# A spectral layer with gated feed-forward on one core: new order of the filter stage, late half evacuations, a moved table load

## The chip, the cores and the metric

The kernel runs on 1 core of one Trainium2 chip. The metric is the device time of one execution in microseconds. The engines are named as in the profile: PE is TensorE, PEld its weight loads, DVE is VectorE, ACT is ScalarE, POOL is GpSimd, SP is SyncE. SP and POOL also issue the DMAs here; SPq and POOLq are their queues.

## The reference, cut to what matters

The input is one sequence of 2048 rows with 576 columns in bf16. First comes a layer norm, a two-dimensional real FFT over rows and columns, a product with a complex filter, and the inverse FFT; the result is added to the input. Then comes a layer norm and a gated feed-forward network with 4608 hidden columns, added again.

```python
def _A_ref(x, w_r, w_i):
    X = jnp.fft.rfft2(x.astype(jnp.float32), axes=(-2, -1))
    W = w_r + 1j * w_i
    X = X * W
    return jnp.fft.irfft2(X, s=(S, D), axes=(-2, -1)).astype(jnp.bfloat16)

def _B_ref(x, w_gate, w_up, w_down):
    return (_gelu(x @ w_gate) * (x @ w_up)) @ w_down

h = x + _A_ref(_layernorm(x), A_w_r, A_w_i)
h2 = h + _B_ref(_layernorm(h), B_w_gate, B_w_up, B_w_down)
```

## The kernel before, in words

**Infrastructure.** A small class `Prog` records every operation with the keys that it reads and writes, and turns them into semaphore waits. Each engine runs its operations in the order in which they are recorded. So the order of the work is the order of the lists below, and an operation that waits holds up everything behind it on its engine. A DMA is recorded on the queue that issues it, SP or POOL, and holds its place there in the same way.

**Stages.** The 2048 rows are 16 tiles of 128 (index c or n). Stage one (list SEQ1) normalises the rows and transforms them along the row axis into U, grouped in 16 groups of frequencies (index i or g). The filter stage (list SEQF) works group by group. The second block (list SEQ) transforms back, adds to the input, normalises, turns tiles 0 to 3 and starts the feed-forward. Tiles 8 to 15 are transformed back later, between the gate/up matmuls (`def_i`, `def_n`). The feed-forward fills the rest.

**The filter stage.** SEQF is written out by hand. A capital letter is the first part of a step, the small letter the second part and its evacuation from PSUM.

- D and d: the transform along the columns, 4 matmuls and then 6; evacuated to CUS by the engine in DENG[i] (line 650 for the matmuls).
- B: 4 matmuls that combine the rows' parts; evacuated to YS by BENG[i] (line 670).
- T: the filter product on DVE, a large multiply into TP (columns 0 to 255) and a small one into TR (the remaining 32 columns) (line 683).
- V and v: the first inverse step on TP, 8 matmuls each; evacuated to V by the engines in VENG[i], one engine for both banks or one for each (line 691).
- R and r: the same for the remainder columns, one step for four groups, from TR (line 708). R0, R1 and R2 are evacuated to RB by RENG and copied to VR by eight DMAs each, shared between SP and POOL. R3 is evacuated by eight small copies straight into VR.

The evacuations are all recorded by one helper, line 616, and the DMAs by line 242. PSUM has 8 banks, used as 4 pairs. A step takes the pair that has been out of use longest (`FB`, `used`, `busy`).

**The second block.** I and i are the second inverse step of a tile, with the V weights and, at the end of i, with the VR weights (line 839). E is the evacuation to GS (lines 845, 846 and 616). N and o are the inverse transform along the rows with the table IT (line 856), a is the addition to XO on DVE (line 862). s, q and c are the variance, the root and its reciprocal; n is the normalisation to HN (line 890; P in its name puts it on POOL); u and U turn HN on PE (line 908), e is that evacuation to HT. G0 and G1 are the first gate/up matmuls (line 948). The bank pairs are chosen in the same way (`SLOT`, `last`, `held`). The loads of the first gate/up weights are issued on SP at the tokens named in LOADS.

**Where the table comes in.** IT and the identity IDT are loaded on SP early, behind the filter weights WS, the tables VT and DT, and ahead of the small loads `w_zero` of WS.

Of the kernel before, what the change touches and what calls it, by code (L numbers as in the profile page):

```python
# [12 lines left out]
NZ, NY = 5, 3  # L13
ABASE = 1
FF = 4608
NT = 16
# [13 lines left out]
DENG, BENG = ['act', 'dve', 'act', 'act', 'act', 'act', 'act', 'act', 'dve', 'act', 'act', 'act', 'act', 'act', 'act', 'act'], ['act', 'dve', 'act', 'act', 'act', 'act', 'act', 'dve', 'act', 'act', 'act', 'act', 'act', 'act', 'act', 'act']  # L30
LOADS = {".I0": "a0 a1 a2 a3 a4 a5", ".N0": "b0", ".i3": "b1", ".o1": "b2", ".N3": "b3", ".o3": "b4 b5", ".i7": "d"}
RENG = ['dve', 'act', 'act', 'act', 'act']
QR = ((0, 1), (1, 2), (2, 3), (3, 4), (4, 8), (8, 16))
DEF0, DSTEP = 3, 4
SEQ = """I0 I1 I2 i0 E0S i1 E1S i2 E2A N0 I3 o0 i3 N1 I4 o1 a0 E3S N2 o2 a1 s0A q0 i4 a2 s1A I7 c0 N3 E4S q1 s2D i7 I6 o3 E7A i6 c1 N4 o4 a3 q2 E6A c2 N7 I5 o7 a4 n0P N6 s3A a7 i5 n1P n2P q3 c3 o6 u1 U1 u2 E5A u0 U2 a6 n3P e1A e2D U0 N5 u3 e0A o5 a5 U3 G0 e3D G1""".split()

# [10 lines left out]
def build_tables():  # L47
# [106 lines left out]
    assert np.allclose(VN[0, 0], VN[0, 1])  # L154
    T["VTAB"] = np.stack([v if k else v.reshape(128, 4, 16, 4).transpose(0, 1, 3, 2).reshape(128, 256) for v, k in ((VN[0, 0], 1), (VN[0, 0], 0), (VN[1, 0], 1), (VN[1, 1], 1), (VN[1, 0], 0), (VN[1, 1], 0))], 1).reshape(128, -1)

# [175 lines left out]
def _build(nc, A_x, A_w_r, A_w_i, B_w_gate, B_w_up, B_w_down, out):  # L332
# [78 lines left out]
    TR = sb.alloc("TR", [128, 2, 2, 2, 128], BF16)  # L411
    RB = sb.alloc("RB", [128, 3, 2, 2, 4, NT], BF16)

# [18 lines left out]
    P.op(POOL, lambda g: g.memset(EXQ[:, :], -0.5), w=["EXQ"])  # L432
    P.op(POOL, lambda g: g.memset(VR[:, :, :, :, :], 0.0), w=[("V", g, 2 + t) for g in range(NG) for t in range(2)])
    xv = A_x[0].rearrange("(p c) d -> p c d", c=NT)
# [105 lines left out]
    def a_bank(i, k):  # L540
        return (5 * i + AORD.index(k) + ABASE) % 8

# [57 lines left out]

    FB, used, busy = {}, {0: -8, 2: -7, 4: -6, 6: -5}, set()
    for t, w in enumerate(SEQF):
# [83 lines left out]
    def st_V(i, second, engs):  # L686
        g, z, b0 = GORD[i], i % NZ, FB["V", i]

        def mm(h, o, ct, first, last, after):
            c, t_ = ct  # L690
            return P.op(PE, lambda t: t.matmul(bank(b0 + o, 0, 128, 128 * c, 128 * c + 128), TP[64 * h:64 * h + 64, z, o, t_, c:256:2], VT[64 * h:64 * h + 64, 0 if g else 2 + o, t_, :],  # L691
                                               start=first, stop=last), r=[("T", z), "VT" if g else "VT2"], w=[("PS", b0 + o)], after=after)

        halves(("V", i), second, [[(c, t_) for c in range(2) for t_ in range(2)]] * 2, mm)
        if not second:
            return
        v5 = V[:, :, :, :, g, :, :].rearrange("p c t n j e -> p j (c t n) e")
        n = 2 // len(engs)
        for a, e in enumerate(engs):
            ev(e, v5[:, n * a:n * a + n], banks(b0 + a, n, 256).rearrange("p a (c e) -> p a c e", e=4), [("PS", b0 + a + k) for k in range(n)], [("V", g, a + k) for k in range(n)])  # L700

    def st_R(q, second):
# [12 lines left out]
        if q < 3:  # L715
            ev(RENG[q], RB[:, q, :, :, :, :].rearrange("p t o e n -> p o t (e n)"), banks(b0, 2, 128).rearrange("p o (t x) -> p o t x", t=2), keys, [("RB", q)])
            for j, i in enumerate(js):
                for t_ in range(2):
                    k = t_ if q == 2 else (2 * j + t_) % 3 > 0
                    P.dma((SP, POOL)[k], VR[64 * t_ + 32 * (j % 2):64 * t_ + 32 * (j % 2) + 32, GORD[i], :, :, :], RB[32 * j:32 * j + 32, q, t_, :, :, :], f"r{q}{k:d}", r=[("RB", q)], w=[("V", GORD[i], 2 + t_)])  # L720
            return
        for i in js:
            j, g = i % 4, GORD[i]
            for t_ in range(2):
                dst = VR[64 * t_ + 32 * (j % 2):64 * t_ + 32 * (j % 2) + 32, g, :, :, :].rearrange("p o e n -> p o (e n)")
                src = PS[32 * j:32 * j + 32, b0 * 512:(b0 + 2) * 512].rearrange("p (a c) -> p a c", a=2)[:, :, 128 * (i == LAST) + 64 * t_:128 * (i == LAST) + 64 * t_ + 64]
                ev((ACT, DVE, DVE, ACT)[j], dst, src, keys, [("V", g, 2 + t_)])

# [33 lines left out]
    def hold(eng=SP):  # L762
        P.op(eng, None, after=[P.ops[PE][-1]])

    def tab2_load():
# [13 lines left out]
    def loads(w):  # L779
        for v in LOADS.get(w, "").split():  # L780
            if v == "d":
                tab2_load()
            else:
                wg0_part(int(v[1]), *((0, 256, ["WGA"]) if v[0] == "a" else (256, 1152, [("WG", 0, i) for i in range(4)])))
# [24 lines left out]
    vk = [vmain, vmain, vtail]  # L809
    vkeys = vmain + vtail  # L810


    SLOT, last, held, ing = {}, [sorted(used.values()).index(used[2 * b]) - 4 for b in range(4)], set(), False
    for t, w in enumerate(SEQ):
# [6 lines left out]
        elif k in "ioUEae":  # L821
# [11 lines left out]
    def i_mm(c, second):  # L833
        b, e = SLOT["I", c], ends.setdefault(("I", c), [None, None])
        for j in range(2 + second):
            for r in range(2):
                o, r0 = r ^ (not second), 64 * r
                lhs = V[r0:r0 + 64, j, o, c, :, :, :] if j < 2 else VR[r0:r0 + 64, :, :, :, c].rearrange("p g o e -> p (g o e)")
                e[o] = P.op(PE, lambda t, r0=r0, o=o, j=j, lhs=lhs: t.matmul(bank(b + o, 0, 128, 0, KW), lhs, DT[r0:r0 + 64, 2 * o + j if j < 2 else 4, 0:KW], start=(not second and j == 0), stop=(second and j == 2)),  # L839
# [120 lines left out]
    def gu_first(i):  # L960
        for a in range(4):
# [29 lines left out]
    def def_i(c, second):  # L991
        e = ends.setdefault(("X", c), [None, None])
        for j in range(3):
            for r in range(2):
                o, r0 = r ^ (not second), 64 * r
                t_ = j if j < 2 else r
                lhs, rhs = (V[r0:r0 + 64, o, t_, c, :, :, :], DP[r0:r0 + 64, 2 * o + t_, :]) if j < 2 else (VR[r0:r0 + 64, :, :, :, c].rearrange("p g o e -> p (g o e)"), DP[r0:r0 + 64, 4 + o, :])
                e[o] = P.op(PE, lambda t, o=o, t_=t_, lhs=lhs, rhs=rhs, j=j: t.matmul(bank(6 + o, 0, 128, HK * t_, HK * t_ + HK), lhs, rhs, start=(not second and j == 0), stop=(second and j == 2)),  # L998
                            r=vk[o if j < 2 else 2] + ["DP"], w=[("PS", 6 + o)], after=[e[o]] if second and j == 0 else [])
        if not second:  # L1000
# [133 lines left out]
```

## Time and profile before

| what | us |
|---|---|
| median of 3 runs | 485.5 (485.09 to 485.71) |
| profiled execution, its own time | 484.82 |
| span of the profile | 483.0 |
| PE busy | 476.7 |
| DVE busy | 183.2 |
| ACT busy | 145.4 |
| POOL busy | 51.2 |

The profile is of one execution. Its span is from the first to the last instruction; the execution's own time is a little longer. A line of the chain of waits has the start, the length and what held the end up in that time. A line of a timeline has start, length, engine, source line, operation, output and inputs, shape, count, and in brackets the idle time before it with what ended it. In a group, busy time and the mean of one instruction in ns stand behind the bar, then the idle time before.

### The profile page before, as it was taken

Reading aid. Unit: us, or ns where it says so; the run is one execution under the profiler, and the core shown is the slowest. Engines: PE = TensorE matmul, PEld = TensorE weight load, DVE = VectorE, ACT = ScalarE, POOL = GpSimd, SP = SyncE. Lnnn points to the kernel's source line nnn. Section 1 sums busy time; section 2 is a strip of 40 time slices with the busy share of each in tenths; the row PEclk is TensorE's granted clock in tenths of the full one; section 3 lists DMA queues with packets and bytes.
Section 4 is the critical chain, followed back from the end, with each engine's and each line's share of the span. In section 5 each row is a group of like instructions: output and inputs, shape, how many; then the busy total and the mean of one; then the engine's idle time right before and its main releaser. Section 6 shows DMA issues by size and latency. Waiting matters only on the chain.

```text
span 483.0 us, 12887 instructions
## 1 busy us (share of the span) xinstructions
PE 476.7 (99%) x5873; PEld 289.0 (60%) x5874; DVE 183.2 (38%) x366; ACT 145.4 (30%) x291; POOL 51.2 (11%) x86
## 2 busy tenths in 40 slices
PE   7999999999999999999999999999999999999998
PEld 3877755555588644444688544444788444445884
DVE  7998655565500143333200244333101233333011
ACT  6998753434300022332100122233000232223000
POOL 7753317010120000000000000000000000000000
PEclk9999999999999999999999999999999999999999
DMA  8883878951520001000000011000000000000000
GB/s 292 226 219 70 278 248 289 375 104 27 195 88 17 26 18 23 18 1 0 3 14 15 26 24 23 12 0 2 3 14 27 14 1 0 1 1 1 3 26 26
DMA packets 28454, 33.19 MB, mean 69 GB/s; under 512 B 12656, under 2 KB 21488, under 8 KB 28400
## 3 DMA queue, kind: packets, MB, share of 16 engines
q1 hardware_dynamic: 24768, 19.88, 14.6%
q0 software_dynamic: 3632, 12.49, 7.9%
q8 instruction: 46, 0.75, 0.7%
q14 instruction: 8, 0.07, 0.0%
HBM read 26.21 MB, written 2.36 MB: 59 GB/s over the span
## 4 chain that ended last, share of the span: by engine, by line
PE 96%; DVE 1%; DMA 1%; POOL 1%; issue 0%; SPq 0%; POOLq 0%; DVEq 0%
PE PS L948 58%; PE PS L1048 27%; PE PS L650 2%; PE PS L1060 2%; PE PS L691 2%; PE PS L561 1%; DMA XO<-in_A_x_dram 1%; PE PS L670 1%; PE PS L839 1%; PE PS L998 1%; DVE XO L862 1%; PE PS L1015 0%; PE PS L856 0%; POOL XN L577 0%; POOL ATS L530 0%
## 5 line engine op out<-in xcount | busy, mean ns | idle before, releaser
L948 PE MATMUL PS<-HT,WG 64*128 64x512 bf16 (+1 forms) x2142 | 233.4, 372 | 0.1
L948 PEld LDWEIGHTS PS<-HT,WG 64*128 64x128 bf16 x2142 | 109.2, 94 | 111.1 <-DMA WG<-in_B_w_up_dram 0.2
L956 ACT ACTIVATE GL<-PS 128x512 bf16<-128x512 f32 x144 | 85.7, 596 | 281.8 <-PE PS L948 281.8
L957 DVE TENSOR_TENSOR AT<-GL,PS 128x512 bf16<-128x512 bf16 x144 | 98.8, 687 | 166.0 <-ACT GL L956 166.0
L1048 PE MATMUL PS<-WD,AT 64*128 64x288 bf16 x2160 | 133.0, 283 | 0.0
L1048 PEld LDWEIGHTS PS<-WD,AT 64*128 64x128 bf16 x2160 | 107.9, 94 | 25.2
L1035 DVE TENSOR_TENSOR OS<-PS,XO 128x288 bf16<-128x288 f32 (+2 forms) x32 | 13.2, 452 | 125.5 <-PE PS L1048 118.0
L948 PE MATMUL PS<-HT,WGX 64*128 64x512 bf16 x486 | 53.4, 376 | 0.0
L948 PEld LDWEIGHTS PS<-HT,WGX 64*128 64x128 bf16 x486 | 24.3, 94 | 28.2
L865 ACT ACTIVATE OS<-XO,NM 128x576 bf16<-128x576 bf16 x15 | 11.6, 773 | 11.4 <-DVE XO L1019 11.4
L650 PE MATMUL PS<-FT,U 64*128 64x288 bf16 x160 | 13.3, 283 | 0.0
L683 DVE TENSOR_TENSOR TP<-YS,WS 128x1024 bf16<-128x1024 bf16 x16 | 11.0, 686 | 0.9 <-DMA WS<-WS 0.6
L504 DVE BATCH_NORM_STATS2 ST<-XO 128x6 f32<-128x288 bf16 x26 | 10.1, 440 | 2.0 <-DMA XO<-in_A_x_dram 2.0
L691 PE MATMUL PS<-VT,TP 64*128 64x128 bf16 x256 | 10.0, 217 | 0.0
L242 POOL DMA_DIRECT2D WG<-in_B_w_gate_dram x9 | 6.1, 679 | 34.4 <-DMA WG<-in_B_w_gate_dram 31.0
L572 ACT ACTIVATE U<-PS 128x384 bf16<-128x384 f32 (+2 forms) x27 | 9.4, 485 | 0.7 <-PE PS L561 0.7
L561 PE MATMUL PS<-ATS,XO 128*128 128x128 bf16 x96 | 8.1, 219 | 1.5 <-POOL ATS L530 1.5
L242 POOL DMA_DIRECT2D WD<-in_B_w_down_dram x9 | 6.7, 755 | 23.8 <-PE PS L1015 23.8
L616 ACT ACTIVATE CUS<-PS 128x576 bf16<-128x576 f32 x14 | 9.0, 656 | 0.3 <-PE PS L650 0.2
L1060 PE MATMUL PS<-WD,AT 128*128 128x448 bf16 (+1 forms) x72 | 9.0, 286 | 0.0
L616 ACT ACTIVATE YS<-PS 128x576 bf16<-128x576 f32 x14 | 8.9, 657 | 0.3
L691 PEld LDWEIGHTS PS<-VT,TP 64*128 64x128 bf16 x256 | 7.9, 94 | 1.4 <-DVE V L616 0.2
(89 smaller groups left out, 227.9 us busy)
## 6 DMA issues: line engine op xcount, KB each, us to landing
WD<-in_B_w_down_dram POOLq DMA_DIRECT2D x9, 576.0 KB, 12.1
WG<-in_B_w_up_dram SPq DMA_DIRECT2D x6, 576.0 KB, 7.1
WG<-in_B_w_gate_dram POOLq DMA_DIRECT2D x6, 576.0 KB, 6.3
out_dram<-OS SPq DMA_DIRECT2D x30, 72.0 KB, 1.7
XO<-in_A_x_dram SPq DMA_DIRECT2D x6, 288.0 KB, 4.8
WGX<-in_B_w_up_dram SPq DMA_DIRECT2D x2, 576.0 KB, 4.4
WGX<-in_B_w_gate_dram POOLq DMA_DIRECT2D x2, 576.0 KB, 5.5
HT<-HN SPq DMA_TRANSPOSE x60, 2.4
```

What stands on the lines that cost most here:

```text
L242: fn = lambda e: e.dma_start(out_ap, in_ap)
L561: P.op(PE, lambda t, b=b, lhs=lhs, p0=p0, p1=p1, s=s, e=e, o=o, c=c: t.matmul(bank(b, p0, p1, o, o + 128), lhs, ATS[:, c, :], start=s, sto ...
L616: fn = (lambda v: v.tensor_copy(dst, src)) if eng == DVE else (lambda a: a.activation(dst, src, ACTF.Copy))
L650: return P.op(PE, lambda t: t.matmul(bank(b0 + o, 0, 128, 0, 2 * HK), U[64 * h:64 * h + 64, us, 2 * i:2 * i + 2, :, :], FT[64 * h:64 * h + ...
L691: return P.op(PE, lambda t: t.matmul(bank(b0 + o, 0, 128, 128 * c, 128 * c + 128), TP[64 * h:64 * h + 64, z, o, t_, c:256:2], VT[64 * h:64 ...
L865: P.op(ACT, lambda a, c=c, out=out: a.activation(out, XO[:, c, 0:D], ACTF.Square, bias=NM[:, c:c + 1], accum_out=SB2[:, 1, c:c + 1]), r=[( ...
L948: op = P.op(PE, lambda t, h0=h0, kt=kt, wt=wt, b=b, s=(not second and j == 0), e=(second and j == n - 1): t.matmul(bank(b, 0, 128, c0, c1) ...
L956: P.op(ACT, lambda a: a.activation(GL[:, s2, :], bank(b0), ACTF.Gelu_apprx_tanh), r=[("PS", b0)], w=[("GL", s2)])
L957: P.op(DVE, lambda v: v.tensor_tensor(AT[:, f, :], GL[:, s2, :], bank(b0 + 1), op=ALU.mult), r=[("GL", s2), ("PS", b0 + 1)], w=[("AT", f)])
L1035: P.op(DVE, lambda v: v.tensor_tensor(OS[:, p % 2, d0:d1], bank(b, 0, 128, 0, d1 - d0), XO[:, c, d0:d1], op=ALU.add), r=[("PS", b), ("X", ...
L1048: e[h] = P.op(PE, lambda t, f=f, h=h, r0=r0, j=j: t.matmul(bank(b0 + h, 0, 128, 0, 288), AT[r0:r0 + 64, f, 128 * p:128 * p + 128], WD[r0:r ...
L1060: P.op(PE, lambda t, b=b, d0=d0, d1=d1, f=f, j=j: t.matmul(bank(b, 0, 128, 0, d1 - d0), AT[:, f, 128 * p:128 * p + 128], WD[:, f, d0:d1], ...
```

## The change

It does these things:

- SEQF has a new order; R2 stands further ahead of the last V steps. DENG, BENG, VENG and RENG give other groups to DVE and ACT.
- The last V (group 15) and R3 are evacuated in two halves. The half for tiles 0 to 7 is copied at once. The half for tiles 8 to 15 is copied at the tokens l15 and l3 of SEQ. VR gets a dimension for the two halves. The late half of R3 goes through RB and eight DMAs on POOL. The two bank pairs are held until these tokens.
- In SEQ, l15 stands behind i0 and l3 behind I3, and I2 moves from before i0 to behind E0S.
- The loads of IT and IDT move on SP to the token R1 of SEQF.
- The eight copies of R0 and of R1 are shared five to SP and three to POOL instead of three and five. Each copy now writes two chunks of 128 bytes in a partition instead of one of 256.
- PAIR renames the bank pairs in stage one and at the start of the filter stage.

```diff
+PAIR = (2, 1, 0, 3)
-SEQF = """D2 D0 d2 D1 d0 d1 B2 D5 B0 d5 T2 D3 B1 d3 D4 T0 T1 B5 d4 D8 B3 d8 D7 T3 B4 d7 V0 D6 v0 V1 T5 d6 v1 R0 V2 r0 v2 T4 B6 D9 B8 T6 V3 d9 D11 v3 d11 B7 D10 B9 d10 V6 V4 T7 v6 v4 V5 B10 v5 R1 D12 T8 r1 d12 B11 T9 V7 D14 v7 T10 d14 D13 B12 d13 D15 T11 V9 T12 d15 v9 V8 B13 v8 R2 r2 T13 B14 T14 B15 V12 V10 v12 v10 V13 V11 T15 v13 V14 v11 v14 V15 R3 v15 r3""".split()
-VENG = [('act',), ('act', 'dve'), ('act', 'dve'), ('act', 'dve'), ('act', 'dve'), ('dve',), ('act', 'dve'), ('act', 'dve'), ('dve',), ('act', 'dve'), ('act',), ('dve',), ('act',), ('act', 'dve'), ('act',), ('act', 'dve')]
-DENG: dve for groups 1, 8; BENG: dve for 1, 7 (all others act)
+SEQF = """D2 D0 d2 D1 d0 d1 B2 D5 B0 d5 T2 D3 B1 d3 D4 T0 B5 d4 D6 T1 B3 d6 D8 B4 d8 V1 V0 T3 v1 v0 D7 B6 T5 d7 V3 V2 v3 R0 v2 r0 D10 T4 B7 d10 T7 D9 B8 d9 V5 D11 v5 T6 B10 d11 V7 V4 v7 V6 v4 R1 v6 r1 D12 B9 T8 T10 d12 D14 B11 d14 D13 V10 d13 D15 v10 T9 T11 B12 d15 R2 r2 T12 B13 V8 B14 v8 V9 T13 B15 v9 V12 T14 V11 v11 V13 v12 T15 V14 v13 v14 V15 R3 v15 r3""".split()
+VENG = [('dve',), ('act',), ('act',), ('act', 'dve'), ('act', 'dve'), ('act', 'dve'), ('act', 'dve'), ('act', 'dve'), ('act', 'dve'), ('act',), ('act',), ('act',), ('act',), ('act', 'dve'), ('act',), ('act', 'dve')]
+DENG: dve for groups 1, 6, 10; BENG: dve for 1, 12 (all others act)
-RENG = ['dve', 'act', 'act', 'act', 'act']
+RENG = ['act', 'act', 'dve', 'act', 'act']
+LOADS = {"R1": "t", ...}
-SEQ = """I0 I1 I2 i0 E0S i1 E1S i2 E2A N0 I3 o0 i3 N1 I4 ...
+SEQ = """I0 I1 i0 l15 E0S I2 i1 E1S i2 E2A N0 I3 l3 o0 i3 N1 I4 ...
...
-    VR = sb.alloc("VR", [128, NG, 2, 4, NT], BF16)
+    VR = sb.alloc("VR", [128, 2, NG, 2, 4, NT // 2], BF16)
...
-    P.dma(SP, IT[:, :, :, :].rearrange("p a b c -> p (a b c)"), dram["ITAB"][:, :], "it", w=["IT"])
-    P.dma(SP, IDT[:, :], dram["EYE"][:, :], "eye", w=["IDT"])
...
+        if i == LAST:
+            v_half(i, 0, ("V", g))
+            return
...
+    def v_half(i, k, key):
+        for a, e in enumerate((ACT, DVE)):
+            src = bank(FB["V", i] + a, 0, 128, 0, 256).rearrange("p (q x) -> p q x", q=4)[:, :, 32 * k:32 * k + 32].rearrange("p q (n e) -> p q n e", e=4)
+            ev(e, V[:, :, :, 8 * k:8 * k + 8, GORD[i], a, :].rearrange("p c t n e -> p (c t) n e"), src, [("PS", FB["V", i] + a)], [(*key, a)])
...
-                    k = t_ if q == 2 else (2 * j + t_) % 3 > 0
+                    k = t_ ^ (j % 2) if q == 2 else (2 * j + t_) % 3 == 1
...
+    def tail_late(q, engs):
+        b0 = FB["R", 3]
+        for p0, p1, c, e in ((0, 96, 0, engs[0]), (96, 128, 128, engs[1])):
+            ev(ENG[e], RB[p0:p1, 0, :, 1, :, :].rearrange("p t o x -> p o t x"), PS[p0:p1, ...],
+               [("PS", b0), ("PS", b0 + 1)], [("RB", 0, p0)])
+        for i in range(12, 16):
+            for t_ in range(2):
+                j = i % 4
+                P.dma(POOL, tail_place(i, t_, 1), RB[32 * j:32 * j + 32, 0, t_, 1, :, :].rearrange("p o x -> p (o x)"), "rl", r=[("RB", 0, 96 if i == LAST else 0)], w=[("VL", GORD[i], 2 + t_)])
...
+    def it_load():
+        P.dma(SP, IT[...], dram["ITAB"][:, :], "it", w=["IT"])
+        P.dma(SP, IDT[:, :], dram["EYE"][:, :], "eye", w=["IDT"])
...
-    SLOT, last, held, ing = {}, [...], set(), False
+    SLOT, last, held, ing = {}, [...], {FB["R", 3] // 2, FB["V", LAST] // 2}, False
...
+        elif k == "l":
+            held.discard(FB["R" if i == 3 else "V", i] // 2)
...
+           "l": lambda q: tail_late(q, "AD") if q == 3 else v_half(q, 1, ("VM", GORD[q]))
```

The order of the columns in the tables VTAB for the remainder, and the keys that the later readers name, follow the new layout.

More of the change, by code (lines that the diff above doesn't have):

```diff
@@ L33 @@
+RENG = ['act', 'act', 'dve', 'act', 'act']
 QR = ((0, 1), (1, 2), (2, 3), (3, 4), (4, 8), (8, 16))
 DEF0, DSTEP = 3, 4
-SEQ = """I0 I1 I2 i0 E0S i1 E1S i2 E2A N0 I3 o0 i3 N1 I4 o1 a0 E3S N2 o2 a1 s0A q0 i4 a2 s1A I7 c0 N3 E4S q1 s2D i7 I6 o3 E7A i6 c1 N4 o4 a3 q2 E6A c2 N7 I5 o7 a4 n0P N6 s3A a7 i5 n1P n2P q3 c3 o6 u1 U1 u2 E5A u0 U2 a6 n3P e1A e2D U0 N5 u3 e0A o5 a5 U3 G0 e3D G1""".split()
+SEQ = """I0 I1 i0 l15 E0S I2 i1 E1S i2 E2A N0 I3 l3 o0 i3 N1 I4 o1 a0 E3S N2 o2 a1 s0A q0 i4 a2 s1A I7 c0 N3 E4S q1 s2D i7 I6 o3 E7A i6 c1 N4 o4 a3 q2 E6A c2 N7 I5 o7 a4 n0P N6 s3A a7 i5 n1P n2P q3 c3 o6 u1 U1 u2 E5A u0 U2 a6 n3P e1A e2D U0 N5 u3 e0A o5 a5 U3 G0 e3D G1""".split()
@@ L432, in _build @@
     P.op(POOL, lambda g: g.memset(EXQ[:, :], -0.5), w=["EXQ"])
-    P.op(POOL, lambda g: g.memset(VR[:, :, :, :, :], 0.0), w=[("V", g, 2 + t) for g in range(NG) for t in range(2)])
+    P.op(POOL, lambda g: g.memset(VR[:, :, :, :, :, :], 0.0), w=[(k, g, 2 + t) for k in ("V", "VL") for g in range(NG) for t in range(2)])
     xv = A_x[0].rearrange("(p c) d -> p c d", c=NT)
@@ L540, in a_bank @@
     def a_bank(i, k):
-        return (5 * i + AORD.index(k) + ABASE) % 8
+        b = (5 * i + AORD.index(k) + ABASE) % 8
+        return 2 * PAIR[b // 2] + b % 2
     def idle_mm(a):
@@ L599, in _build @@
     LAST = NG - 1
-    FB, used, busy = {}, {0: -8, 2: -7, 4: -6, 6: -5}, set()
+    FB, used, busy = {}, {2 * PAIR[k]: k - 8 for k in range(4)}, set()
     for t, w in enumerate(SEQF):
@@ L780, in loads @@
         for v in LOADS.get(w, "").split():
-            if v == "d":
-                tab2_load()
+            if v in "td":
+                (it_load if v == "t" else tab2_load)()
             else:
@@ L809, in _build @@
     vk = [vmain, vmain, vtail]
-    vkeys = vmain + vtail
-    SLOT, last, held, ing = {}, [sorted(used.values()).index(used[2 * b]) - 4 for b in range(4)], set(), False
+    vlate = [("VM", GORD[LAST], a) for a in range(2)] + [("VL", GORD[i], 2 + t) for i in range(12, NG) for t in range(2)]
+    vkeys = vmain + vtail + vlate
+    SLOT, last, held, ing = {}, [sorted(used.values()).index(used[2 * b]) - 4 for b in range(4)], {FB["R", 3] // 2, FB["V", LAST] // 2}, False
     for t, w in enumerate(SEQ):
@@ L996, in def_i @@
                 t_ = j if j < 2 else r
-                lhs, rhs = (V[r0:r0 + 64, o, t_, c, :, :, :], DP[r0:r0 + 64, 2 * o + t_, :]) if j < 2 else (VR[r0:r0 + 64, :, :, :, c].rearrange("p g o e -> p (g o e)"), DP[r0:r0 + 64, 4 + o, :])
+                lhs, rhs = (V[r0:r0 + 64, o, t_, c, :, :, :], DP[r0:r0 + 64, 2 * o + t_, :]) if j < 2 else (VR[r0:r0 + 64, c // 8, :, :, :, c % 8].rearrange("p g o e -> p (g o e)"), DP[r0:r0 + 64, 4 + o, :])
                 e[o] = P.op(PE, lambda t, o=o, t_=t_, lhs=lhs, rhs=rhs, j=j: t.matmul(bank(6 + o, 0, 128, HK * t_, HK * t_ + HK), lhs, rhs, start=(not second and j == 0), stop=(second and j == 2)),
-                            r=vk[o if j < 2 else 2] + ["DP"], w=[("PS", 6 + o)], after=[e[o]] if second and j == 0 else [])
+                            r=(vk[o] if j < 2 else vtail) + vlate + ["DP"], w=[("PS", 6 + o)], after=[e[o]] if second and j == 0 else [])
         if not second:
```

29 lines of the change are left out of this document (17 added, 12 removed).

## The prediction

> **What bounds the kernel now.** I read the page first, then the chain of waits over the whole span, then the windows of the filter stage, the groups by form, and the timelines of each queue from 18 to 56 us.
>
> ```profile
> span 483.0 us, 12887 instructions
> PE 476.7 (99%) x5873; PEld 289.0 (60%) x5874; DVE 183.2 (38%) x366; ACT 145.4 (30%) x291; POOL 51.2 (11%) x86
> ```
>
> TensorE (PE) is busy 476.7 of 483.0 us, so only the few microseconds in which it waits or is held back can be won. The chain says where they are:
>
> ```profile
> 18.90 1.97 PE PS L650 x30
> 22.28 0.24 PE PS L670 x4
> 22.53 0.61 PE PS L650 x10
> 36.47 0.22 PE PS L691 x8
> 37.99 0.20 PE PS L708 x4
> 41.94 0.24 PE PS L691 x8
> 42.17 0.42 DVE V L616
> 42.60 0.14 issue
> 43.89 0.06 issue
> 43.95 1.08 PE PS L839 x14
> 45.86 0.76 DVE XO L862
> 54.33 6.35 PE PS L948 x92
> 60.68 0.19 PE PS L998 x6
> ```
>
> The filter stage (the SEQF list) runs from 18.90 to 42.17. Call the second time T0: the last V matmul has ended and block 15's evacuation starts. The second block (the SEQ list) follows until G0, the first gate/up matmul, at 54.33, which is T0 + 12.16. From G0 to the end the chain is TensorE without a gap, and the change issues nothing there that it did not issue before; only the VR weights are read with another stride, beside matmuls (six of them 0.19 us at 60.68), which I cost at nothing. So the change is worth the shift of G0, and that is the shift of T0 plus the change of those 12.16 us.
>
> **The filter stage.** The rows give the stage's unit costs on PE: a D step 0.61, a B 0.24, half a V 0.22 (8 matmuls). Both orders have 16 D, 16 B, 16 V and 4 R. Until V15 ends that is 16 x 0.61 + 16 x 0.24 + 32 x 0.22 + the R halves (32 matmuls, four times 0.22) = 21.5 us, against 42.17 - 18.90 = 23.27. No order can gain more than 1.75 us here. It loses them because two other engines are nearly as full:
>
> ```profile
> 20.00:40.00 20.00, 19.93 (x430) 15.07 (x426) 18.77 (x45) 19.42 (x39) 13.48 (x28) 1.00 0.72 187
> L616 ACT ACTIVATE CUS<-PS 128x576 bf16<-128x576 f32 x14 | 9.0, 656 | 0.3 <-PE PS L650 0.2
> L616 ACT ACTIVATE V<-PS 128x512 bf16<-128x512 f32 x4 | 2.3, 607 | 0.2 <-PE PS L691 0.2
> L616 ACT ACTIVATE V<-PS 128x256 bf16<-128x256 f32 x9 | 3.4, 392 | 0.2
> L616 ACT ACTIVATE VR<-PS 32x128 bf16<-32x128 f32 x4 | 1.1, 264 | 0.0
> L616 DVE CAST CUS<-PS 128x576 bf16<-128x576 f32 x2 | 1.5, 750 | 0.0
> L616 DVE CAST V<-PS 128x512 bf16<-128x512 f32 x3 | 2.1, 684 | 0.1
> L616 DVE CAST V<-PS 128x256 bf16<-128x256 f32 x9 | 3.7, 415 | 0.1
> L616 DVE CAST VR<-PS 32x128 bf16<-32x128 f32 x4 | 1.1, 286 | 0.1
> 39.59 0.68 DVE L683 TENSOR_TENSOR TP<-YS,WS 128x1024 bf16<-128x1024 bf16 x1
> 40.33 0.69 DVE L683 TENSOR_TENSOR TP<-YS,WS 128x1024 bf16<-128x1024 bf16 x1
> ```
>
> In the window the columns are PE, PEld, DVE, ACT, POOL: of 20 us DVE works 18.77 and ACT 19.42. The new engine lists give DVE a third D (+0.75) but only one whole V and seven halves instead of three and nine, and a half-length V15: 0.684 + 7 x 0.415 + 0.286 against 3 x 0.684 + 9 x 0.415, that is -1.91. A 256-element copy takes 0.415 and a 128-element one 0.286, so 1.0 ns an element, and a 64-element piece is estimated at 0.22; the four R3 pieces save 0.26. DVE: -1.4 us. ACT loses one D (-0.66), takes seven whole V instead of four and seven halves instead of nine plus the half V15 (+1.30), and saves about 0.25 on R3: +0.4 us. The load goes from DVE, which has some room, to ACT, which has least. B and R0 to R2 only change places.
>
> The end of the new list is what I cost in detail, because DVE has a fixed queue there: YS of B12, RB of R2, T12, half V8, T13, T14, T15, and V15 cannot start before T15. A T step is 0.74 (39.59 to 40.33), a little less than its parts because an operation starts about 0.08 before its predecessor ends. With that step the queue is 0.68 + 0.33 + 0.74 + 0.33 + 0.74 + 0.74 + 0.69 = 4.25 us. PE has only 0.37 + 0.22 + 3 x 0.24 + 6 x 0.44 = 3.95 us between B12 and V15, so DVE sets the end. When does B12 end? Up to it PE has 15 x 0.61 + 0.24 + 13 x 0.24 + 9 x 0.44 + 0.44 = 16.91 us of work. In the old order PE reached R2 at 37.99 after 17.96 us of work, 1.13 behind. At that rate B12 ends at 36.87, with half of the lag at 36.3. I take 36.6, nearer the first: ACT is the fuller engine and gets more. Then 0.24 until DVE takes it, 4.25, 0.14 back to PE (the issue row), three halves of 0.22 (V15, R3, V15) and 0.14 to the evacuation: T0 = 42.03, 0.14 earlier. Bounds: 0.45 earlier, 0.4 later if ACT's extra 0.4 us all shows.
>
> **The inverse table.** IT and the identity leave SP's queue ahead of the small WS loads and go between the R0 and R1 copies. There the load costs nothing if it lands before N0, near 44.8:
>
> ```profile
> IT<-c_itab SPq DMA_DIRECT2D x1, 512.0 KB, 6.1
> L242 SPq DMA_DIRECT2D VR<-RB x10: 507/592/1352, 28.2 to 41.5; - x10
> DMA to landing us min/median/max: 1.6/2.3/5.0
> ```
>
> R0's evacuation comes near 28.9 in either order; SP then issues five copies instead of three (0.59 each in the median, 1.35 at most), then the table, by about 33 to 35: landed by 41. Cover 4 us. What it passes is R1's and R2's copies, and that is a rival below. The copies' two 128-byte chunks instead of one of 256 I cost at nothing: they are off the chain as long as R2's land in time. The renamed bank pairs alone are a relabelling, at nothing.
>
> **The turn into the second block.** Times are from T0.
>
> ```profile
> 42.62 1.19 DVE L616 CAST VR<-PS 32x128 bf16<-32x128 f32 x4
> 44.31 0.82 DVE L845 CAST GS<-PS 128x288 bf16<-128x288 f32 x2 [0.51 <-PE PS L839]
> 45.07 0.65 ACT L616 ACTIVATE GS<-PS 128x576 bf16<-128x576 f32 x1
> 45.16 0.42 PE L839 MATMUL PS<-DT,V 64*128 64x288 bf16 x4
> ```
>
> Before: V15 is evacuated at +0.42, I0 starts at +0.56, the four R3 pieces on DVE end at 43.81, and the VR part of i0 starts at 43.95, +1.78. After: half of V15 takes 0.29, I0 starts at +0.43, the four 64-element pieces (0.236 each with their gap) end at +1.27, the VR part starts at +1.41. So 0.37 us is gained here. But I2 now takes V15's bank pair, which is free only after l15, the late half, on DVE until +1.56; I2 starts at +1.70 where PE would be free at +1.54. I2, i1, i2 and N0 need 0.24 + 0.36 + 0.36 + 0.24 and bring PE to +2.90. I3 takes I1's pair, which is free after E1S (i1 issued at +2.30, evacuated from +2.50 to +2.95): I3 at +3.09. Before it started at 45.16, +2.99. The 0.37 us is therefore given back by the two pair waits, and a0 on DVE, after which DVE runs its old chain back to back, comes 0.10 later relative to T0.
>
> **The late copies on POOL.** This is the term that decides.
>
> ```profile
> 39.23 1.96 POOL L242 DMA_DIRECT2D VR<-RB  x4 [0.27 <-ACT RB L616]
> 48.64 0.86 POOL L890 TENSOR_SCALAR HN<-XO,NM,RS 128x640 bf16<-128x640 bf16 x1 [7.45 <-DVE RS L875]
> 50.30 0.87 POOL L890 TENSOR_SCALAR HN<-XO,NM,RS 128x640 bf16<-128x640 bf16 x1 [0.80 <-DVE RS L875]
> 51.34 0.87 POOL L890 TENSOR_SCALAR HN<-XO,NM,RS 128x640 bf16<-128x640 bf16 x1 [0.17 <-POOL HN L890]
> 52.54 0.87 POOL L890 TENSOR_SCALAR HN<-XO,NM,RS 128x640 bf16<-128x640 bf16 x1 [0.32 <-DVE RS L875]
> 53.61 0.26 PE L908 MATMUL PS<-IDT,HN 64*128 64x64 bf16 x6
> ```
>
> l3 copies the late R3 halves to RB, on ACT behind E2A (45.07 + 0.65, +3.55): 128 elements, 0.264, done at +3.75. POOL wakes 0.27 later and issues eight DMAs at 0.49 (1.96 for four): +4.02 to +7.94. Behind them on POOL stand n0 to n3, the normalisations of tiles 0 to 3, which PE turns in u0 to u3. Before, POOL idled 7.45 us ahead of n0 and ran it at +6.47. Now n0 starts near +8.02 and four of 0.87 with three gaps of 0.17 end at +12.01, against 53.41, +11.24, before. u3 came 0.20 after n3 and G0 0.72 after u3. So G0 is at +12.93 instead of +12.16: 0.77 later.
>
> The sum: -0.14 + 0.77 = +0.6 us. The copies themselves are needed first at 60.68 and land by about 52.5, so they cost nothing else. The profiled execution took 484.82, its span 483.0; it would become 485.4 with a span of 483.6. It lies 0.7 below the median of the runs, so I put the difference on the median: 485.5 + 0.6 = 486.1.
>
> A rule that speaks against these copies: the Trainium skill, page "SBUF — State Buffer", section "A bandwidth-pool intuition that's wrong (but worth ruling out)", says that a DMA issued from GpSimd that takes about 620 ns alone takes about 3100 ns while VectorE runs a copy, because descriptors cannot be written meanwhile. By that figure eight issues would be an estimated 25 us and G0 some 21 us late. Here four issues took 1.96 us in a stretch in which DVE ran T steps and PSUM copies without a pause, so the trace does not show it for DVE work of this kind.
>
> **The rivals.** 0.2% is 0.97 us, about what a measurement of this kernel can tell from no change.
>
> - POOL does not bind (0.18). If n2 and n3 are not what u2 and u3 wait for, only the pair waits remain: -0.14 + 0.10, about 485.5. For it: before, u3 stood behind N5 and not clearly behind n3. Against: n3 ends 0.77 later in my sum, and u3 had 0.20.
> - The filter ends later (0.16). ACT, at 19.42 of 20, gets 0.4 more; if that shows, T0 comes 0.4 later and G0 +1.2: 486.7, slower. It decides if ACT has no pause of 0.4 us left in the new order. Against: PE still waits 1.75 us in the stage.
> - R2's copies land late (0.11). SP has 14 copies and two tables where it had 10 copies. At the median issue R1's five are done by 37 and R2's last lands near 42.4, an estimate; i0's VR part wants it at T0 + 1.41 = 43.44. If most issues take the 1.35 us of the maximum, it lands a microsecond late or more, and everything behind it moves: +0.6 + 1.1, 487.2, slower.
> - Dearer POOL issues (0.05).
>
> ```profile
> L242 POOL DMA_DIRECT2D WG<-in_B_w_gate_dram x9 | 6.1, 679 | 34.4 <-DMA WG<-in_B_w_gate_dram 31.0
> ```
>
>   Weight loads take POOL 0.679 an issue. At that price the eight take 1.5 us more: 487.6.
> - The new order wins most of the 1.75 us (0.10). If T0 comes 1.2 earlier, with POOL not binding, G0 is 1.1 to 1.2 earlier: 484.3, faster. It needs ACT and DVE to feed PE almost without a wait, and T15 to come 1 us sooner than its DVE queue allows from a B12 at 36.6.
>
> **How the numbers follow.** The forecast has 0.40, and 486.1 is its time; its own range, by the bounds of T0, is 485.8 to 486.6. Within 0.2% are it and the first rival: 0.58. Slower are the second, third and fourth: 0.32. Faster is the last: 0.10. The range is 485.0 to 487.0: it takes in the forecast, the free POOL case with T0 up to 0.45 early, and the late filter, and leaves out the faster case and most of the two dearest.
>
> **What would show it.** Right: G0 between 54.7 and 55.2; T0 near 42.0 with V15 waiting for the TP multiply of T15; eight POOL issues of 0.49 from about 46.0 and n0 straight behind them with no idle time; u2 and u3 waiting for POOL's HN; I3 waiting for the evacuation of I1. Wrong: POOL idle ahead of n0; T0 below 41.4 or above 42.5; the VR part of i0 later than T0 + 1.6, waiting for a DMA; any change behind G0.

## The result, and the profile after

The changed kernel takes 486.28 us in the median of 22 runs, the kernel before 485.44 in 22 runs beside it. The ratio is 1.0017 with a 95% interval of 1.0010 to 1.0023: about 0.8 us slower. The forecast was 486.1, 0.6 us slower, with a range of 485.0 to 487.0, and the measured time lies inside it. The terms of its sum, however, were not the ones that the trace shows.

The profiled execution has a span of 484.2 us, 1.2 more than before. First the page and the window of the filter stage (columns as before: PE, PEld, DVE, ACT, POOL):

```profile
span 484.2 us, 12906 instructions
PE 477.5 (99%) x5873; PEld 328.3 (68%) x5874; DVE 183.0 (38%) x366; ACT 146.2 (30%) x294; POOL 52.9 (11%) x90
20.00:40.00 20.00, 19.65 (x426) 14.68 (x420) 18.71 (x44) 19.50 (x39) 11.76 (x25) 1.00 0.77 191
```

DVE and ACT are as full as before (18.77 and 19.42 then); the window is too full to show the work that has gone from DVE to ACT. The chain of waits from the end of the filter stage to G0 shows where the time stands now:

```profile
42.44 0.28 DVE V L616
...
44.00 0.39 issue
44.39 0.97 PE PS L868 x12
...
46.40 0.17 ACT RB L616
46.57 0.28 issue
46.85 3.08 POOL VR L243 x7
...
50.82 0.88 POOL HN L919
...
53.96 0.88 POOL HN L919
54.84 0.14 issue
54.98 0.26 PE PS L937 x6
```

Before, the chain ran from the filter over DVE's additions (DVE XO) to PE. Now it goes through POOL: eight copies and, straight behind them, four normalisations with pauses of at most 0.18, then u3 on PE. T0 is 42.43, the VR part of i0 starts at 44.39, a0 at 46.57 and G0 at 55.50. One more row belongs to the reading: on SP the last nine copies, those of R1 and R2, follow the table.

```profile
34.61 0.59 SPq L243 DMA_DIRECT2D IT<-c_itab  x1
35.24 0.43 SPq L243 DMA_DIRECT2D IDT<-c_eye  x1
35.71 7.00 SPq L243 DMA_DIRECT2D VR<-RB  x9
44.39 0.34 PE L868 MATMUL PS<-DT,VR 64*128 64x288 bf16 x2 [0.61 <-DVE V L616]
```

The bracket blames DVE's late half of V15, which i0 doesn't read. The event was another one: R2's last copy on SP, issued from 42.11 to 42.71, landed at 43.89, and the VR part started 0.50 later.

All profiles are compared by the same marks, in us. D0 is the first D matmul (18.8 to 19.4 everywhere), VR the VR part of i0, a0 the first addition. From G0 to the end every profile takes the same 428.7 (428.65 to 428.80), except the last one of the table. The last column is the ratio of the runs to runs of the kernel before on the same chip, with its 95% interval; all ratios lie within 0.5% of 1, so a difference counts only where the intervals leave room for it. Full names of the runs stand with the experiments.

| profile | T0 - D0 | R2 landed - T0 | VR - T0 | a0 - T0 | G0 - a0 | G0 - D0 | ratio |
|---|---|---|---|---|---|---|---|
| before | 23.33 | 1.18 | 1.79 | 3.70 | 8.47 | 35.50 | 1 |
| after | 23.55 | 1.46 | 1.96 | 4.14 | 8.93 | 36.62 | 1.0017 [1.0010, 1.0023] |
| x1 no late copies | 23.13 | 2.43 | 2.89 | 5.06 | 8.47 | 36.66 | 1.0001 [0.9992, 1.0011] |
| x2 old shares | 23.13 | 0.54 | 1.39 | 3.66 | 8.92 | 35.70 | 0.9993 [0.9985, 1.0002] |
| x3 both of these | 23.12 | 0.58 | 1.39 | 3.65 | 8.47 | 35.24 | 0.9982 [0.9974, 0.9991] |
| x4 YS of B12 on ACT | 23.65 | 1.54 | 2.05 | 4.22 | 8.93 | 36.80 | 1.0011 [1.0003, 1.0020] |
| x5 split copies | 23.82 | 0.94 | 1.39 | 3.66 | 8.47 | 35.95 | 0.9983 [0.9975, 0.9992] |
| x6 order alone | 23.11 | 0.26 | 1.79 | 3.70 | 8.52 | 35.32 | 0.9989 [0.9980, 0.9999] |
| x7 late halves alone | 24.10 | 1.44 | 1.90 | 4.08 | 9.86 | 38.03 | 1.0041 [1.0027, 1.0055] |
| x8 table early | 23.64 | 0.36 | 1.39 | 3.65 | 8.91 | 36.21 | 1.0001 [0.9993, 1.0009] |
| x9 tables on POOL | 23.21 | 0.41 | 1.39 | 3.66 | 8.47 | 35.34 | 0.9995 [0.9985, 1.0005] |
| x10 V15 whole | 23.12 | 0.32 | 1.55 | 3.45 | 8.47 | 35.05 | 0.9982 [0.9971, 0.9993] |
| x11 late halves, pairs renamed | 23.32 | 1.44 | 1.90 | 4.08 | 8.93 | 36.33 | 1.0018 [1.0009, 1.0028] |
| x12 x9 and x10 together | 23.13 | 1.11 | 1.66 | 3.59 | 8.47 | 35.18 | 0.9995 [0.9986, 1.0004] |

By these marks the 1.12 us by which G0 - D0 grew is +0.22 in the filter stage, +0.44 from T0 to a0 and +0.46 from a0 to G0.

### The profile page after: what moved, and what is told of

Read it like the earlier page. It is cut to its first block, busy times and chain, and to the rows that moved or that the text cites. A ratio compares the mean times of both kernels' runs of the same rounds, so it can differ in the third digit from the quotient of the medians.

```text
span 484.2 us, 12906 instructions
## 1 busy us (share of the span) xinstructions
PE 477.5 (99%) x5873; PEld 328.3 (68%) x5874; DVE 183.0 (38%) x366; ACT 146.2 (30%) x294; POOL 52.9 (11%) x90
## 4 chain that ended last, share of the span: by engine, by line
PE 90%; SPq 4%; DMA 2%; POOL 2%; issue 1%; DVE 1%; ACT 0%; POOLq 0%; DVEq 0%
PE PS L977 58%; PE PS L1077 27%; SPq L243 4%; PE PS L1089 2%; DMA WS<-in_A_w_r_dram 1%; DMA WS<-WS 1%; PE PS L691 1%; POOL VR L243 1%; POOL HN L919 1%; PE PS L1027 1%; PE PS L1044 0%; DVE TP L683 0%; PE PS L650 0%; PE PS L670 0%; PE PS L868 0%
## 5 line engine op out<-in xcount | busy, mean ns | idle before, releaser
L977 PEld LDWEIGHTS PS<-HT,WG 64*128 64x128 bf16 x2142 | 125.6, 94 | 94.8 <-DVE AT L986 0.2
L1077 PEld LDWEIGHTS PS<-WD,AT 64*128 64x128 bf16 x2160 | 126.6, 94 | 6.4
L977 PEld LDWEIGHTS PS<-HT,WGX 64*128 64x128 bf16 x486 | 28.5, 94 | 23.9
L243 POOL DMA_DIRECT2D VR<-RB x18 | 9.2, 519 | 9.2 <-ACT RB L616 6.2
```

The lines of the kernel that those rows point to most:

```text
L243: fn = lambda e: e.dma_start(out_ap, in_ap)
L977: op = P.op(PE, lambda t, h0=h0, kt=kt, wt=wt, b=b, s=(not second and j == 0), e=(second and j == n - 1): t.matmul(bank(b, 0, 128, c0, c1) ...
L1077: e[h] = P.op(PE, lambda t, f=f, h=h, r0=r0, j=j: t.matmul(bank(b0 + h, 0, 128, 0, 288), AT[r0:r0 + 64, f, 128 * p:128 * p + 128], WD[r0:r ...
```

## The experiments

Each run is the changed kernel with the edit shown, unless it says otherwise. x1 to x4, x5 to x8 and x9 to x12 ran on three chips, four runs on each, timed in five rounds.

### The late copies and the shares (x1, x2, x3)

The theories: the eight late copies hold POOL up and G0 with it (forecast); R2's copies land late because SP has more of them (a rival). x1 takes the copies away, x2 gives SP and POOL their old shares, x3 does both.

```diff
 x1 and x3:
-                P.dma(POOL, tail_place(i, t_, 1), RB[32 * j:32 * j + 32, 0, t_, 1, :, :]..., "rl", ...)
+                pass
 x2 and x3:
-                    k = t_ ^ (j % 2) if q == 2 else (2 * j + t_) % 3 == 1
+                    k = t_ if q == 2 else (2 * j + t_) % 3 > 0
```

> The changed kernel without the eight DMAs that bring the late R3 halves from RB to VR; so the remainder columns of groups 13, 14, 15 and 0 are missing from tiles 8 to 15. Theory A (the copies stand ahead of n0 to n3 on POOL and set G0): n0 starts as soon as its reciprocal is there, near 49.3 instead of 50.82, and G0 is held only by what comes earlier: a0 is 0.71 later than in the kernel before (46.57 against 45.86), so G0 near 55.0 instead of 55.50, and the time about 0.5 us under the changed kernel. Rival B (POOL does not bind, G0 follows from a0 and the chain on DVE alone): G0 stays within 0.1 of 55.5.

> The changed kernel with the copies of R0, R1 and R2 shared between SP and POOL as in the kernel before (three and five of eight instead of five and three). Theory C (SP's queue is too long, R2's last copy lands at 43.89, after the R3 pieces are done at 43.67, and holds i0's VR part until 44.39): SP issues R2's last copy a microsecond sooner, it lands before 43.2, the VR part starts near 43.85, everything behind moves 0.5 earlier: G0 near 55.0. Rival (the landing is not what holds the VR part, the many semaphores that PE has to look at are): the VR part stays near 44.3 and G0 near 55.4.

> Both edits of the two runs before: no late copies (same columns missing) and the old shares. If A and C are both right and add up, a0 is near 46.05, G0 near 54.5 to 54.6, about 0.9 to 1.0 us under the changed kernel, which is 485.3 to 485.4, the time of the kernel before; what is left against it is the later end of the filter stage (0.27) less what the half evacuations win. If only one of them binds, it is no better than the better of the two.

Both theories hold, one beside the other. The chain of x1 no longer goes through POOL, and G0 - a0 falls from 8.93 to 8.47, the value of before. But it opens with SP and a landing:

```profile
41.97 0.60 SPq L243
...
42.61 1.77 DMA VR<-RB
44.39 0.46 issue
44.84 1.32 PE PS L868 x18
...
55.03 0.34 PE PS L885 x4
...
55.49 2.56 PE PS L977 x43
```

The matmuls at 44.84 start with the VR part of i0: it waits for the copy that SP issued at 42.61, the last of R2 (the row at 41.97 is the issue before it). In this execution it landed at T0 + 2.43, so a0 was late by 1.4 us against x3. That is why G0 stands at 55.49, the very time that rival B had named: the two effects happen to cancel, and only the marks tell them apart. x2 has the opposite half: R2 lands at T0 + 0.54, the VR part starts at T0 + 1.39 and a0 stands at T0 + 3.66, but POOL is still in the chain:

```profile
50.80 1.49 DVE XO L891 x2
52.29 0.08 DVE RS L904
52.38 0.11 issue
52.48 0.88 POOL HN L919
...
53.53 0.88 POOL HN L919
54.41 0.14 issue
54.55 0.26 PE PS L937 x6
```

x3 has neither, and is 0.18% faster than before: with both costs gone the change is a gain. It came 0.7 us sooner than expected; 0.4 of that is the late filter stage of the profile after (23.55), which the expectation had carried over and x3's profile doesn't have (23.12).

### Two more readings of the filter stage (x4, x8)

x4 gives the YS evacuation of B12 from DVE to ACT, to see whether DVE's queue sets T15, as the prediction had it. x8 puts the table back to its early place.

```diff
 x4, in BENG:
-'act', 'dve', 'act', 'act', 'act']     (group 12 on dve)
+'act', 'act', 'act', 'act', 'act']     (group 12 on act)
 x8:
-LOADS = {"R1": "t", ".I0": ...
+LOADS = {".I0": ...
+    P.dma(SP, IT[...], dram["ITAB"][:, :], "it", w=["IT"])      behind the load of DT
+    P.dma(SP, IDT[:, :], dram["EYE"][:, :], "eye", w=["IDT"])
```

> The changed kernel with group 12's YS evacuated by ACT instead of DVE, one entry of BENG. If DVE's queue from YS12 to T15 sets the end of the filter stage, as the prediction has it, that queue is 0.68 shorter, T15's multiply ends up to 0.6 sooner than 41.39 and T0 comes 0.2 to 0.4 sooner than 42.43. If ACT is the full engine there, its extra 0.55 us shows and T0 is the same or up to 0.4 later.

> The changed kernel with the inverse table and the identity loaded early again, as before; five of eight R0 and R1 copies stay on SP, eight late copies on POOL. Theory C: without the two table issues between the copies SP issues R2's last copy up to 1.0 us sooner, it lands before the R3 pieces are done, a0 comes 3.65 to 3.8 after T0 instead of 4.14 and the time is near 485.5 to 485.8. If the table is not what makes SP late, but the ten copies instead of six, R2's last copy still lands 24.8 or more after the first D and nothing is won.

x4 went against the theory: T0 - D0 is 23.65, though no TP multiply waited for a transfer in its profile; the other profiles of the new order with no such wait have 23.11 to 23.21. The window from 36 to 42 us of x4 and two rows of its DVE tell why:

```profile
36.00:42.00 6.00, 5.64 (x153) 4.41 (x148) 4.67 (x13) 6.00 (x14) 2.10 (x4) 1.00 0.34 103
38.88 0.42 DVE L616 CAST V<-PS 128x256 bf16<-128x256 f32 x1 [0.32 <-PE PS L691]
39.22 0.69 DVE L683 TENSOR_TENSOR TP<-YS,WS 128x1024 bf16<-128x1024 bf16 x1
```

In x4 ACT is busy for 6.00 of 6.00 us and DVE for 4.67, with a pause of 0.32 (and one of 0.88 ahead of R2's evacuation) in the very queue that I had taken for the bound. With 0.68 us less to do DVE did not end earlier: in x4 ACT sets the pace. That doesn't hold for the changed kernel itself. There the same window and the two ends of DVE's queue are:

```profile
36.00:42.00 6.00, 5.87 (x159) 4.82 (x156) 5.75 (x16) 5.72 (x13) 2.11 (x4) 1.00 0.40 106
37.05 0.76 DVE L616 CAST YS<-PS 128x576 bf16<-128x576 f32 x1
40.70 0.69 DVE L683 TENSOR_TENSOR TP<-YS,WS 128x1024 bf16<-128x1024 bf16 x1
```

From the YS of B12 at 37.05 to the end of T15's multiply at 41.39 DVE has no pause, and V15 starts 0.15 later, at 41.54. In every profile of the new order but x4 it is so, except for a pause of 0.08 in x5. PE comes to V15 at about the same time (its matmul before starts at 41.44). So DVE sets the end there, by little, and ACT is so close behind that one YS more on it costs 0.5 in the profile of x4; the runs (1.0011 against 1.0017) don't show x4 slower than the change.

In x8 R2 lands at T0 + 0.36 and a0 stands at T0 + 3.65. From D0, R2's last copy lands at 25.01 to 25.56 in the three profiles of the new order that have both the change's shares and the table at R1 (after, x1, x4), and at 23.4 to 24.8 in the eight that lack one or both. So either edit takes most of the lateness away in the mean (23.85 against 25.25); the scatter of about 1.4 us stays.

### The parts alone (x6, x7, x11)

x6 is the new order, engines, table place and PAIR, with V15 and R3 evacuated whole, the old start of SEQ and the old shares. x7 is the late halves (with l15, l3 and the POOL copies) on the lists, the table place, the shares and the pairs of before. x11 is x7 with the pairs renamed so that each block of the second block has the pair that it has in the changed kernel.

```diff
 x7, against the change:
-PAIR = (2, 1, 0, 3)
+PAIR = (0, 1, 2, 3)
 x11, against x7:
-PAIR = (0, 1, 2, 3)
+PAIR = (3, 0, 2, 1)
```

> The new order, engine lists, table load and bank names alone: V15 and R3 evacuated whole as in the kernel before, the old SEQ, the old shares. If the order by itself wins what the runs so far show, T0 comes 23.1 after the first D matmul instead of 23.3, the turn takes 3.70 to a0 as before, G0 follows by 8.47: about 0.2 us under the kernel before, near 485.3. If the new order wins only together with the short evacuations, T0 is at 23.3 or later and there is no gain.

> The late halves alone: the order, engines, table load, shares and bank names of the kernel before, with V15 and R3 evacuated in halves, l15 and l3 in SEQ, and the eight late copies on POOL. Theory A: T0 as before, 23.3 after the first D; a0 3.65 to 3.75 after T0; G0 8.9 after a0 instead of 8.47 since n0 to n3 stand behind the copies: 0.4 to 0.5 us over the kernel before, near 486.0. If the halves win 0.3 us or more at the turn, as their shorter pieces alone would have it (VR part 1.4 instead of 1.78 after T0), it is no slower than before.

> The late halves on the old order, as in the run with the late halves alone, but with the pairs renamed to (3, 0, 2, 1), so that every block of the second stage has the pair that it has in the changed kernel: N5 on pair 3 (banks 6 and 7) instead of pair 0. Theory (the renaming is needed by the late halves: on pair 0 the sum of tile 5 must be read before G0 can write banks 0 and 1): G0 - a0 is 8.9 instead of 9.86, and the chain has no DVE XO ahead of G0; 0.95 us less than the run without the renaming, a ratio of 1.002 where that had 1.0041. Rival (bank names are a relabelling at nothing, and the 0.95 came from the old order): 9.8 and 1.004 stay.

The order alone is a small gain, 0.11%, with an interval that just leaves out 1. The late halves alone are a loss, and a larger one than I expected until the pairs are renamed. The ends of the two chains, x7 first:

```profile
55.71 0.26 PE PS L887 x4
...
55.99 0.77 DVE XO L893
...
56.90 1.14 PE PS L979 x17
```

```profile
54.90 0.25 PE PS L887 x4
55.14 0.06 PE PS L939 x4
55.20 2.84 PE PS L979 x49
```

In x7 the held pairs push N5 onto pair 0, whose banks 0 and 1 G0 writes. So G0 waits until DVE has added tile 5. In x11 N5 is on pair 3, the addition leaves the chain, and G0 - a0 is 8.93 instead of 9.86. In the profiles the rest of the gap lies in the filter stage (24.10 against 23.32), where but for the names of the banks the two do the same: in x7 the TP multiply at 27.13 waits 0.83, in x11 none waits so long. The profile puts that wait down to PE, but a copy of filter weights landed 0.08 before the multiply, as at the wait of 0.45 at the same step in before. Waits of this kind are taken up below, with the filter stage.

x11 also shows R2 late, at T0 + 1.44, with the old shares and the old table place. In before it landed at T0 + 1.18 and held nothing up, since DVE worked on R3's pieces until T0 + 1.64. The late halves shorten those pieces to T0 + 1.24 and so uncover it.

### Mending it (x5, x10, x9, x12)

x5 leaves nothing out: old shares, four late copies on POOL, and the other four on SP behind the weight loads at the token o3. x10 is x5 with V15 evacuated whole again, so that only R3's pair is held. x9 is x5 with the tables VT2, DT, IT and IDT issued by POOL at the token R1. x12 is x9 and x10 together.

```diff
 x5, besides the old shares:
-                P.dma(POOL, tail_place(i, t_, 1), ...)
+                if t_ == 0:
+                    P.dma(POOL, tail_place(i, t_, 1), ...)
...
+    def late_sp():                     (called behind the loads of ".o3")
+        for i in range(12, 16):
+            t_, j = 1, i % 4
+            P.dma(SP, tail_place(i, t_, 1), ..., "rs", ...)
 x10, besides x5:
-SEQ = """I0 I1 i0 l15 E0S I2 i1 E1S ...
+SEQ = """I0 I1 I2 i0 E0S i1 E1S ...
-        if i == LAST:
-            v_half(i, 0, ("V", g))
-            return
 x9, besides x5 (VT and DT stood early on SP, IT and IDT at "R1"; now all at "R1"):
-    P.dma(SP, VT[...], "vt2"); P.dma(SP, DT[...], "dt"); P.dma(SP, IT[...], "it"); P.dma(SP, IDT[...], "eye")
+    P.dma(POOL, VT[...], "vt2"); P.dma(POOL, DT[...], "dt"); P.dma(POOL, IT[...], "it"); P.dma(POOL, IDT[...], "eye")
```

> The whole computation again: the changed kernel with the old shares of the R0 to R2 copies, and the eight late copies split: four on POOL where they were, four on SP behind the last part of the first weight load, when SP has nothing to do. Theory A: four POOL issues end near 48.4, before n0's reciprocal is there, so POOL no longer costs anything: G0 follows a0 by 8.47 as without the copies, against 8.93 with all eight on POOL; a0 follows T0 by 3.65. G0 comes 35.2 to 35.3 after the first D matmul, as in the run with both edits, and the time is 484.6 to 484.8, about 0.8 us under the kernel before. Rival: SP's four copies land too late and hold the activation tiles that take over RB's place, or n0 still waits: then G0 is as in the run with the old shares alone, 35.7 after the first D, 485.1, or worse.

> The split version with block 15 evacuated whole again and the old start of the second block (I0 I1 I2 i0); only R3 keeps its late half. Theory (the wait of I2 for the pair of V15 and of I3 for that of I1 gives the gain of the late halves back): V15's evacuation takes 0.13 more, the R3 pieces end at T0 + 1.37, the VR part is at T0 + 1.52, no pair wait follows, and a0 stands 1.91 after the VR part as before the change, at T0 + 3.43, 0.2 earlier than the 3.65 of the split, where it is 2.27 after it. Rival (the pair waits are hidden by the evacuations E0 to E2): a0 stays 2.27 after the VR part, at T0 + 3.79. In time that is a ratio of 0.998 or 0.9985, too near to each other to tell; the marks of the profile decide.

> The split version with the four tables VT2, DT, IT and the identity issued by POOL behind its R0 copies, none by SP. Theory (the tables on SP delay R2's copies, and their transfers beside the filter loads delay the WS<-WS copies for which T8 waited in three profiles): T8 follows its DVE queue, T0 - D0 is 23.1 as in the profiles in which T8 did not wait; R2's last copy lands before T0 + 0.9, the VR part of i0 is at T0 + 1.39, a0 at T0 + 3.65, G0 at a0 + 8.47, so G0 - D0 is 35.2 against 35.95 in the profile of the split and 35.50 before. The median is 0.3 to 0.6 us below the split's ratio of 0.9983: 0.997 to 0.9977. Rival (T8's wait is chance, not the tables): the copy's landing still moves between profiles, T0 - D0 anywhere from 23.1 to 23.8, and the ratio stays at 0.998 to 0.9985.

> Both edits on the split: the tables on POOL and block 15 whole. If both theories hold, T0 - D0 is 23.1, a0 at T0 + 3.43, G0 at a0 + 8.47: G0 - D0 35.0, 0.5 less than before and 1.6 less than after the change, a ratio of 0.9965 to 0.9975. If the pair waits are hidden, it is 0.1 slower than the run with the tables alone, 35.35; if T8's wait is chance, it may come out as the split did, 0.998.

x5 beats both kernels: G0 - a0 is 8.47, as without any late copy, so four copies fit into POOL's pause ahead of n0 and eight don't. x10 settles what the pair waits cost. Its chain after T0:

```profile
42.08 0.42 DVE V L616
...
42.64 2.03 PE PS L871 x30
44.67 0.30 PE PS L888 x4
44.97 0.27 PE PS L871 x4
45.24 0.26 PE PS L888 x4
45.52 0.76 DVE XO L894
```

V15 takes 0.42 instead of 0.29 and the VR part starts 0.16 later, yet a0 comes at T0 + 3.45, 0.21 earlier than in x5. Once the VR part can start, a0 follows it by 1.90, as in before (1.91), where x5 needs 2.27. So 0.37 us are what l15 and the new start of SEQ, with I2 waiting for V15's pair, give back together; x10 leaves both out at once. x10 has the shortest G0 - D0 of all, 35.05, and a ratio of 0.9982; against x5's 0.9983 the time can't tell them apart.

x9 does in its profile what was expected (no wait of a TP multiply for a transfer, R2 at T0 + 0.41, G0 - D0 35.34), but not in its time: 0.9995, which neither the theory nor its rival had named and which is no gain over x5, and x12 has the same. In x12 R2 is late once more, at T0 + 1.11, and a new wait stands behind G0:

```profile
51.86 6.68 DMA WG<-in_B_w_up_dram
...
58.59 1.47 PE PS L980 x11
```

The last part of the first gate/up weights landed late for the matmuls, and from G0 to the end x12 takes 0.34 us more than the others. Whether that is also what ate the gain of x9 in its other executions stays open: its own profile doesn't have it.

## Why the prediction was right or wrong

**The filter stage.** Forecast -0.14; measured +0.22 in the profile of the change. The order itself does what was forecast: six profiles of it (x1, x2, x3, x6, x10, x12) have T0 - D0 at 23.11 to 23.13, which is -0.2 and inside the bounds. The reason given for it holds too: DVE's queue from B12 to T15 takes 4.34 (forecast 4.25) and V15 starts 0.15 behind it (forecast 0.14). The step that failed is a term that was put at nothing, a wait that depends on the execution. T steps read copies of the filter weights that POOL moves within SBUF (WS<-WS), and in some profiles one isn't there in time. Changed kernel, then x10:

```profile
33.88 0.69 DVE L683 TENSOR_TENSOR TP<-YS,WS 128x1024 bf16<-128x1024 bf16 x1 [0.33 <-DMA WS<-WS]
```

```profile
33.53 0.68 DVE L683 TENSOR_TENSOR TP<-YS,WS 128x1024 bf16<-128x1024 bf16 x1
```

The waits for these copies sum to 0.33 us in the profile after, 0.43 in x8 and 0.59 in x5, and T0 - D0 exceeds 23.12 by 0.43, 0.52 and 0.70 there. In the old order they sum to 0.4 in x11 and to 1.2 in x7. The kernel before has them too, 0.6 in two waits, which I had read over. x5 and x10 have one filter stage in common, and T0 - D0 is 23.82 in the one and 23.12 in the other: this term can't be had from one profile to better than some 0.7 us. The rival with the full ACT is not what made the stage later: the six profiles have its 0.4 us more on ACT as well. x4 shows that it was near.

**The turn.** Forecast +0.10, measured +0.44. Without the lateness of R2 the step holds to 0.15: the VR part at T0 + 1.39 (forecast 1.41) and a0 at T0 + 3.65, which is -0.05. The pair waits that I set against the earlier start are shown by x10. The rest, +0.49, is the rival with R2's late copies, to which I gave 0.11, as a case by itself; it happened together with the forecast's own case. The step that failed is the time of that landing: I had let them land near 42.4, and they landed at 43.89. SP took 7.00 us for its last nine copies, 0.78 each, not the median of 0.59, and stood behind a table. The cover was also shorter than I counted: the copy must be there 0.46 to 0.55 before the VR part starts, in each of the profiles in which it is late (after, x1, x4, x7, x11, x12).

**POOL.** Forecast +0.67 from a0 to G0 (12.93 - 12.16 less the 0.10 of a0), measured +0.46. The mechanism was the right one, and x1, x3 and x5 against x2, x4 and x8 show it. The POOL part itself was sized right: relative to a0 n3 was to end at +8.21 and ended at +8.26.

```profile
46.85 3.92 POOL L243 DMA_DIRECT2D VR<-RB  x8 [6.22 <-ACT RB L616]
50.82 0.87 POOL L919 TENSOR_SCALAR HN<-XO,NM,RS 128x640 bf16<-128x640 bf16 x1
...
54.98 0.26 PE L937 MATMUL PS<-IDT,HN 64*128 64x64 bf16 x6 [0.16 <-POOL HN L919]
```

The term that was too large is the tail behind n3: I took over 0.20 to u3 and 0.72 from there to G0, and they measured 0.15 and 0.52. In before u3 and G0 did not hang on n3, so part of that 0.92 was slack, and it went first. The eight issues took 0.49 each while DVE ran its additions and its copies out of PSUM, so the rule of the Trainium skill that I set against them (page "SBUF — State Buffer", section "A bandwidth-pool intuition that's wrong (but worth ruling out)") isn't seen in the issues here either. But its figure is the time of a DMA, and I had set it against that of an issue. R2's four copies on POOL landed 2.0 to 2.2 us after their issue though DVE was busy for 2.00 of 2.00 us (38 to 40); the late copies took 3.0 to 6.3, with the weight loads under way beside them, and what stretched them was not tried.

**The rest.** The table cost nothing by itself, as forecast, but something through the queue in which it stands. With the late halves on the old order the renaming is needed, 0.93 us from a0 to G0, and I had called it a relabelling without following N5. With the new order and whole evacuations G0 - a0 is 8.52 against 8.47 before (x6); that order without the renaming was not run. Behind G0 nothing changed.

Of the prediction's own signs of being wrong one came true: the VR part started later than T0 + 1.6, waiting for a DMA, and G0 at 55.50 lies beyond the 54.7 to 55.2 of being right. V15 waiting for T15, the eight issues and n0 straight behind them are as it had them. So the mechanism on POOL was right, and that the number was near is in part luck: forecast -0.14 + 0.10 + 0.67 = +0.6; in the profile 0.22 + 0.44 + 0.46 = +1.1, two terms too small and one too large; and +0.8 in the runs. That the runs lie lower because the landings differ from execution to execution is likely, but not shown. A rival had been needed that joins the forecast's own case to the late copies.

## What to carry to other kernels

Whoever shortens a step on the path should ask which event was hidden behind it: R2's copies were nearly as late before, and only the shorter R3 pieces made them count. A DMA that is issued from a computing engine's queue costs its issue time (here 0.49 each) to everything behind it there, so count the pause ahead of the next due operation (here four issues fit and eight didn't) and split the copies between queues. Where a term hangs on a landing time, take its spread from several profiles before you give it a sign.

## What the runs showed of the hardware

- The issue of a small copy took nearly the same on POOL every time: 0.49 us for the eight late copies (3.92), 0.49 for R2's four in before (1.96), and 0.53 for R2's four in the profile after (2.11), which write two chunks in a partition instead of one. On SP the last nine took 0.78 in the mean (7.00): seven took 0.60, one 1.12 and one 1.35.
- From the landing of a copy to the first matmul that reads it PE needed 0.46 to 0.55 us when the copy was the last event. The profile calls it issue. The sequencer's records show four semaphore waits in a row there, the copy's the first, with starts 0.11 to 0.20 apart, and then the weight load; that they are what takes the time is a reading of the trace that no run tested.
- The WS<-WS copy for which the TP multiply at 33.88 waited lands at 32.3 to 33.9 us in the profiles of the new order. POOL issues it at 26.8 to 29.4, since it waits there for loads that scatter as well (released at 28.35 in after, at 26.94 in x1). What scatters them wasn't tried, except by x9.
